# Seven products for the last block's projection, and an earlier spread of the first block's attention

## Chip, cores and metric

One core of a Trainium2 chip. The metric is the device time of the kernel in microseconds (us); lower is better.

## The reference

```python
# q, k, v: (8 batches, 8 heads, 576 tokens, 64)
scores = q @ k.T / 8 + bias(head, distance), masked to 0 <= distance < 128
x      = softmax(scores) @ v             # heads joined: 4608 tokens x 512
g, val = x @ w_gate, x @ w_val           # 512 -> 1536
out    = (silu(g) * val) @ w_out         # 1536 -> 512, float32
```

## The kernel before

The 4608 tokens are nine blocks of 512 (block 8 is made of the last 64 tokens of all eight batches). For a block, attention makes four tiles `x`, TensorE transposes them (`px`, copied to `xT`), and twelve columns of the FFN follow: a gate group `pg`, a value group `pv` (four matmuls of 512 each), ScalarE's `tt`, VectorE's `uu` and `hT`. Then the block is projected by `w_out` (`po`). In attention, `pt` is the transpose of a tile of k or q (loaded as `kn`, `qn`), `ps` and `psc` are the scores, and `av` is their product with v; the rank of a tile is its place in the order of use. All of it is one list of steps in which attention steps of later blocks are mixed with FFN steps of the present one. A scheduler turns the list into one fixed instruction order for each engine, using its own idea of durations; on the chip each engine then takes its instructions in that order.

How far attention is pushed ahead is the target. `b1` is 24, `ALONE` is 8, so this is one attention step an FFN step from 8, and three from 16:

```python
if step < b1:
    target = base + max(0, step - ALONE) + max(0, step - 16) * (32 - b1 + ALONE) / (b1 - 16)
...
while (n_att < target or done < ready[blk]) and att_step():
    pass
```

The loads are issued by GpSimd. k and q of ranks 9 and 10 are issued later from within the steps, so they stand in the queue behind `w_out` (two loads of 768 KB, issued at 40.36 and 41.83 us; k and q follow from 42.64):

```python
load(7)
load(8)
loaded = 9
for a0 in (0, 6):
    nc.gpsimd.dma_start(wo_sb[:, a0:a0 + 6, :], wo2[:, a0:a0 + 6, :])
```

Block 0 is projected plainly during block 1.

```python
def project(n, j, pool, tag, bufs):
    po = pool.tile([P, DM], FP32, name="po", tag=tag, bufs=bufs)
    for m0 in range(0, NMB, 4):
        for i in range(m0, m0 + 4):
            m = NMB - 1 - i if n == 0 else i
            nc.tensor.matmul(po, hT[n][:, m, j * P:(j + 1) * P], wo_sb[:, m, :],
                             start=(i == 0), stop=(i == NMB - 1))
        ...
```

Blocks 1 to 7 are projected with seven products instead of eight (`strassen`, a Winograd form: halves of tokens, of columns of `hT`, and of columns of `w_out`; `sums` makes the sums of `hT` on VectorE; the code below is condensed, with lines joined and helpers left out). Block 8 was the exception: three tiles by `project`, the last by `last_project` in two halves of 256 columns.

```python
def strassen(n, t):                      # t: one of two halves, called in turn
    po = ps_f.tile([P, 2, HC], FP32, name="po", tag="po", bufs=1)
    ...
    X, Y = po[:, 0, :], po[:, 1, :]      # two accumulators, one tile
    product(X, A11, B11, True);  nc.scalar.mul(p1s, X, 0.5);         yield
    product(p2, A12, B21, True); half_plus(top[:, 0:HC], p2, p1s);   yield
    product(X, S2, T2);          nc.scalar.mul(u2s, X, 0.5);         yield
    product(Y, S1, T1);          nc.scalar.mul(p5s, Y, 0.5);         yield
    product(X, S3, T3);          half_plus(low[:, HC:DM], X, p5s);   yield
    product(Y, S4, B22);         half_plus(top[:, HC:DM], Y, u2s);   yield
    product(X, A22, T4);         nc.scalar.mul(low[:, 0:HC], X, 0.5)
    # stores of top and low
```

The softmax here doesn't subtract the row's maximum and nothing guards it: scores larger than these inputs give would overflow.

Of the kernel before, what the change touches and what calls it, by code (L numbers as in the profile page):

```python
# [10 lines left out]
FP32 = mybir.dt.float32  # L11
# [5 lines left out]
P = 128  # L17
# [4 lines left out]
ALONE = 8  # L22
# [25 lines left out]
def kernel(  # L48
# [10 lines left out]
    nc = tc.nc  # L59
    B, H, S, D = q.shape  # L60
    NTOK, DM = out.shape
    DFF = moe_w_gate.shape[1]
    NKB = DM // P
    NMB = DFF // P
    NSUP = B // 2
    NBLK = NTOK // 512
# [50 lines left out]
    wo_sb = consts.tile([P, NMB, DM], FP16, name="wo_sb")  # L117
# [9 lines left out]
    supool = ctx.enter_context(tc.tile_pool(name="sup", bufs=4))  # L127
    opool = ctx.enter_context(tc.tile_pool(name="op", bufs=8))
    ps_f = ctx.enter_context(tc.tile_pool(name="ps_f", bufs=3, space=PSUM))
    ps_a = ctx.enter_context(tc.tile_pool(name="ps_a", bufs=4, space=PSUM))  # L130
# [225 lines left out]
    hT = {}  # L356
# [36 lines left out]
    def gate_val(n, m):  # L393
        c0 = 384 if (n, m) in acted else 0
        gate(n, m, wide(n, m, "g"), c0)
        yield
        val(n, m, wide(n, m, "v"), c0)
        yield

    def rows_of(n, j):  # L400
        if n == 8:
            return [(0, 64, 2 * j * S + 512), (64, 128, (2 * j + 1) * S + 512)]
        return [(0, 128, n * S + j * P)]

    def project(n, j, pool, tag, bufs):
        po = pool.tile([P, DM], FP32, name="po", tag=tag, bufs=bufs)
        for m0 in range(0, NMB, 4):
# [4 lines that stand above are left out]
            if m0 + 4 == NMB:  # L412
                osb = opool.tile([P, DM], FP32, name="osb", tag="osb")
                nc.scalar.mul(osb, po, 0.5)
                for p0, p1, r0 in rows_of(n, j):
                    nc.sync.dma_start(out[r0:r0 + p1 - p0, :], osb[p0:p1, :])
            yield

    def last_project(n, j):

        osb = opool.tile([P, DM], FP32, name="osb", tag="osb")
        for half in range(2):
            c = slice(half * DM // 2, (half + 1) * DM // 2)
            po = ps_a.tile([P, DM // 2], FP32, name="po", tag="a", bufs=4)
            for m in range(NMB):
                nc.tensor.matmul(po, hT[n][:, m, j * P:(j + 1) * P], wo_sb[:, m, c],
                                 start=(m == 0), stop=(m == NMB - 1))
            if half == 0:
                nc.scalar.mul(osb[:, c], po, 0.5)
            else:  # L430
                nc.vector.tensor_scalar_mul(osb[:, c], po, 0.5)
            for i, (p0, p1, r0) in enumerate(rows_of(n, j)):
                (nc.sync if i == 0 else nc.scalar).dma_start(out[r0:r0 + p1 - p0, c], osb[p0:p1, c])
            yield 1.5



# [2 lines left out]
    HC = DM // 2  # L440
# [4 lines left out]
    def weight_sums(c):  # L445

        if c == 0:
            one_more.append(supool.tile([P, 1], FP32, name="one", tag="pin", bufs=1))
            nc.vector.memset(one_more[0], 1.0)
        k = slice(2 * c, 2 * c + 2)  # L450
        for t_, a, b in ((T1, B12, B11), (T3, B22, B12)):
            nc.vector.scalar_tensor_tensor(out=t_[:, k, :], in0=a[:, k, :], scalar=one_more[0],
                                           in1=b[:, k, :], op0=ALU.mult, op1=ALU.subtract)
        nc.vector.tensor_sub(T2[:, k, :], B22[:, k, :], T1[:, k, :])
        nc.vector.tensor_sub(T4[:, k, :], B21[:, k, :], T2[:, k, :])
# [17 lines left out]
    def strassen(n, t):  # L473

        h = hT[n]
        A11, A12 = h[:, 0:HM, 0:256], h[:, HM:NMB, 0:256]
        S1, A22 = h[:, 0:HM, 256:512], h[:, HM:NMB, 256:512]
        S2, S3, S4 = hsum[n]
        cols = slice(t * P, (t + 1) * P)
        po = ps_f.tile([P, 2, HC], FP32, name="po", tag="po", bufs=1)  # L480
        p2 = ps_a.tile([P, HC], FP32, name="p2", tag="a")
        top, low = (opool.tile([P, DM], FP32, name="osb", tag="osb") for _ in range(2))
        p1s = supool.tile([P, HC], FP32, name="p1s", tag="p1s", bufs=1)
        p5s = supool.tile([P, HC], FP32, name="p5s", tag="p5s", bufs=1)
        u2s = supool.tile([P, HC], FP32, name="u2s", tag="u2s", bufs=1)

        def product(dst, a, b, start=False):
            for m in range(HM):
                nc.tensor.matmul(dst, a[:, m, cols], b[:, m, :], start=(start and m == 0),  # L489
                                 stop=(m == HM - 1), skip_group_check=True)  # L490

        def half_plus(dst, a, b):
            nc.vector.scalar_tensor_tensor(out=dst, in0=a, scalar=0.5, in1=b,
                                           op0=ALU.mult, op1=ALU.add)

        X, Y = po[:, 0, :], po[:, 1, :]
        product(X, A11, B11, True)
        nc.scalar.mul(p1s, X, 0.5)
        yield
        product(p2, A12, B21, True)  # L500
        half_plus(top[:, 0:HC], p2, p1s)
        yield
        product(X, S2, T2)
        nc.scalar.mul(u2s, X, 0.5)
        yield
        product(Y, S1, T1)
        nc.scalar.mul(p5s, Y, 0.5)  # L507
        yield
        product(X, S3, T3)
        half_plus(low[:, HC:DM], X, p5s)  # L510
        yield
        product(Y, S4, B22)
        half_plus(top[:, HC:DM], Y, u2s)
        yield
        product(X, A22, T4)
        nc.scalar.mul(low[:, 0:HC], X, 0.5)
        for j, osb in ((t, top), (t + 2, low)):
            for p0, p1, r0 in rows_of(n, j):
                nc.sync.dma_start(out[r0:r0 + p1 - p0, :], osb[p0:p1, :])
        yield  # L520



    AT = {2, 3, *range(5, 10), *range(11, 18)}
# [1 line left out]
    def ffn():  # L526

        for n in range(NBLK):
            if n > 1:
                parts = chain(strassen(n - 1, 0), strassen(n - 1, 1))  # L530
            if n == 1:
                for j in range(PRE):
                    for _ in project(0, j, ps_f, "po", 1):
                        yield 1.0
            for m in range(NMB):
                for half, _ in enumerate(gate_val(n, m)):
                    yield 1.0
                    if n > 1 and 2 * m + half in AT:
                        next(parts)
                        yield 0.75  # L540
                if n == 1:
                    if m % 2 and PRE + m // 2 < 4:
                        for _ in project(0, PRE + m // 2, ps_f, "po", 1):
                            yield 1.0
                    if m in (2, 4, 6):
                        weight_sums(m // 2 - 1)
                if 0 < n < NBLK - 1 and m >= 9:
                    sums(n, m - 9)
            if n > 1:
                assert next(parts, None) is None  # L550
        for j in range(3):
            for _ in project(NBLK - 1, j, ps_a, "a", 4):
                yield 1.0
        yield from last_project(NBLK - 1, 3)


    loaded = done_t = 0
# [126 lines left out]
    def everything():  # L684
        nonlocal done
        base = 0
        busy(WARM)
        with tc.manual_schedule(engines=ENGINES[MANUAL]):
            first_tiles()
            done = FIRST  # L690
            steps = progress(ffn())
            while (at := next(steps)) < ALONE:
                if at == 2.0:
                    nc.scalar.copy(idm2, idm)
        for step in steps:
            if step == MASKS_AT:
                make_masks()

            b1 = 24 + 3 * PRE

            lead = LEAD if done < X_DMA_FROM - 2 else LEAD + 4
            blk = (0 if step + LEAD < b1 else 1 if step + LEAD < 60
                   else min(NBLK - 1, 2 + int((step + lead - 60) // 34.5)))
            if step < b1:

                target = base + max(0, step - ALONE) + max(0, step - 16) * (32 - b1 + ALONE) / (b1 - 16)
            elif step < 60:
                target = base + 32 + SECOND * 8 * (step - b1) / (60 - b1)
            else:
                target = base + 32 + SECOND * 8 + (step - 60) * RATE * 8 / 34.5  # L710
            while (n_att < target or done < ready[blk]) and att_step():
                pass
# [32 lines left out]
```

## Time and profile before

| | before |
|---|---|
| time, median of 3 runs | 356.27 us (356.26 to 356.39) |
| span in the profile | 354.5 us |
| TensorE busy | 341.5 us, 96% |
| clock granted to TensorE | 1.00 throughout |
| last matmul ends, tail after it | 350.54, 3.92 us |
| first `pg` of block 1 | 56.93 us |

TensorE is the bound, so the tables and lines below are read for two things only: how long TensorE's next instruction waits, and how long the span goes on after its last one. The lines for this are in the prediction.

### The profile page before, as it was taken

The page shows a single profiled execution, that of the slowest core. Times are in us where ns is not written, and L with a number is a line of the kernel's source. Part 1 is how long each engine was busy: PE and PEld are TensorE (multiplying, and loading weights), DVE is VectorE, ACT ScalarE, POOL GpSimd, SP SyncE. Part 2 cuts the span into 40 slices and gives each one's busy share as a digit, 9 for nine tenths or more (in the row PEclk, how much of TensorE's full clock was granted, in tenths as well). Part 3 has the DMA queues.
Part 4 walks back from the last instruction along what each step waited for, and adds up shares of the span by engine and source line. Part 5 has one row for each costly group of instructions (what it writes and reads, how often), then busy time and mean ns, then how long its engine had stood idle before and what let it go on. Part 6 is the DMA issues. An engine that isn't in the chain of part 4 may idle for free.

```text
span 354.5 us, 7261 instructions
## 1 busy us (share of the span) xinstructions
PE 341.5 (96%) x2765; PEld 197.5 (56%) x2765; DVE 273.4 (77%) x599; ACT 178.9 (50%) x355; POOL 106.9 (30%) x132
## 2 busy tenths in 40 slices
PE   7889999999999999999999999999999999999995
PEld 4684555444456655565456555664665566556643
DVE  4867976997987799678986998799878965975540
ACT  6845584555555455665556455455444323332321
POOL 8966655544848445544300100000000000000000
PEclk9999999999999999999999999999999999999999
DMA  9999999999999999999995513311022101101114
GB/s 152 170 186 187 141 176 155 99 147 137 157 142 196 146 158 163 157 167 153 165 62 105 83 39 32 88 33 58 17 75 61 44 2 59 62 0 62 41 42 96
DMA packets 157763, 37.34 MB, mean 105 GB/s; under 512 B 147232, under 2 KB 153248, under 8 KB 157728
## 3 DMA queue, kind: packets, MB, share of 16 engines
q0 software_dynamic: 116224, 18.62, 79.8%
q1 hardware_dynamic: 41056, 17.97, 27.6%
q8 instruction: 21, 0.34, 0.4%
q10 hardware_dynamic: 448, 0.30, 0.3%
q14 instruction: 14, 0.11, 0.1%
HBM read 37.91 MB, written 9.44 MB: 134 GB/s over the span
## 4 chain that ended last, share of the span: by engine, by line
PE 73%; DVE 16%; ACT 7%; issue 3%; DVEq 0%; ACTq 0%
PE pv L369 20%; PE pg L369 20%; PE po L489 14%; PE av L320 4%; DVE uu L384 4%; DVE hT L391 3%; PE ps L255 3%; PE po L410 3%; DVE ex L264 3%; PE p L489 2%; ACT ex L260 2%; PE px L346 2%; ACT tt L383 2%; ACT exc L287 2%; DVE x L323 1%
## 5 line engine op out<-in xcount | busy, mean ns | idle before, releaser
L369 PE MATMUL pg<-xT,wg_sb 128*128 128x512 f16 (+2 forms) x464 | 116.0, 365 | 0.6 <-DVE uu L384 0.3
L369 PE MATMUL pv<-xT,wv_sb 128*128 128x512 f16 (+2 forms) x464 | 114.5, 364 | 0.8 <-DVE uu L384 0.4
L383 ACT ACTIVATE tt<-pg 128x512 f16<-128x512 f32 (+2 forms) x110 | 65.5, 596 | 85.2 <-PE pg L369 81.8
L384 DVE SCALAR_TENSOR_TENSOR uu<-tt,pg 128x512 f16<-128x512 f16 (+2 forms) x109 | 73.4, 674 | 34.6 <-ACT tt L383 33.9
L391 DVE TENSOR_TENSOR hT<-uu,pv 128x512 f16<-128x512 f16 (+2 forms) x110 | 74.0, 673 | 7.1 <-PE pv L369 2.2
L369 PEld LDWEIGHTS <-wv_sb 128*128 128x128 f16 x464 | 42.8, 98 | 37.4 <-issue 3.3
L369 PEld LDWEIGHTS <-wg_sb 128*128 128x128 f16 x464 | 42.5, 98 | 36.1 <-issue 3.5
L260 ACT ACTIVATE ex<-ps 128x512 f16<-128x512 f32 x96 | 50.2, 605 | 10.1 <-PE ps L255 10.1
L169 POOL DMA_DIRECT2D va<-in_v_dram x40 | 34.1, 856 | 53.0 <-PE av L320 36.9
L175 POOL DMA_DIRECT2D qn<-in_q_dram x39 | 33.6, 864 | 24.4 <-DMA qT<-qn 14.8
L175 POOL DMA_DIRECT2D kn<-in_k_dram x39 | 33.2, 859 | 25.7 <-DMA kT<-kn 18.4
L264 DVE TENSOR_TENSOR ex<-ex,m_reg 128x1024 f16<-128x1024 f16 x48 | 32.6, 687 | 10.3 <-ACT ex L260 10.3
L489 PEld LDWEIGHTS <-hT 128*128 128x128 f16 x336 | 31.8, 98 | 15.5 <-issue 3.6
L489 PEld LDWEIGHTS <-S 128*128 128x128 f16 x252 | 23.9, 98 | 11.8 <-issue 2.9
L323 DVE TENSOR_TENSOR x<-av,rec 128x256 f16<-128x256 f32 x72 | 29.0, 420 | 0.6
L489 PE MATMUL po<-T,hT 128*128 128x256 f16 x168 | 23.1, 272 | 0.5
L489 PE MATMUL po<-T,S 128*128 128x256 f16 x168 | 23.0, 273 | 0.6 <-ACT p5s L507 0.6
L287 ACT ACTIVATE exc<-psc 128x512 f16<-128x512 f32 x40 | 21.4, 608 | 3.4 <-PE psc L283 3.4
L347 ACT COPY xT<-px 128x512 f16<-128x512 f16 x24 | 14.1, 586 | 14.9 <-PE px L346 14.8
L320 PEld LDWEIGHTS <-ex 128*128 128x128 f16 x384 | 18.4, 97 | 4.9 <-issue 0.7
L320 PE MATMUL av<-va,ex 128*128 128x65 f16 x384 | 20.4, 193 | 0.5
L410 PE MATMUL po<-wo_sb,hT 128*128 128x512 f16 x84 | 19.7, 379 | 0.0
(74 smaller groups left out, 291.0 us busy)
## 6 DMA issues: line engine op xcount, KB each, us to landing
out_dram<-osb SPq DMA_DIRECT2D x32, 256.0 KB, 2.8
va<-in_v_dram POOLq DMA_DIRECT2D x32, 128.0 KB, 7.5
qn<-in_q_dram POOLq DMA_DIRECT2D x31, 128.0 KB, 8.2
kn<-in_k_dram POOLq DMA_DIRECT2D x31, 128.0 KB, 8.1
wo_sb<-in_moe_w_out_dram POOLq DMA_DIRECT2D x2, 768.0 KB, 9.3
wg_sb<-in_moe_w_gate_dram POOLq DMA_DIRECT2D x2, 512.0 KB, 10.5
wv_sb<-in_moe_w_val_dram POOLq DMA_DIRECT2D x2, 512.0 KB, 11.8
out_dram<-osb SPq DMA_DIRECT2D x6, 128.0 KB, 2.4
```

What stands on the lines that cost most here:

```text
L169: nc.gpsimd.dma_start(va[rank][p0:p1, :, 0:D], src)
L175: nc.gpsimd.dma_start(t_[p0:p1], src)
L260: nc.scalar.activation(e[:, o:o + 2, :], banks[q4][par], AF.Exp, scale=scale)
L264: nc.vector.tensor_mul(e[:, o, :], e[:, o, :], reg[:, o, :])
L320: nc.tensor.matmul(av[:, j, :], w, val, start=(n == 0), stop=(n == len(todo) - 1))
L323: nc.vector.tensor_mul(x[:, 4 * half:4 * half + 4, :], av[:, :, 0:D], rec.broadcast_to([P, 4, D]))
L369: nc.tensor.matmul(ps[:, c0:c1], w[:, kb, ms], xT[n][:, kb, c0:c1], start=(kb == 0 and c0 == 0), stop=(kb == NKB - 1 and c1 == 512), skip_ ...
L383: nc.scalar.activation(tt, pg[:, c0:c1], AF.Tanh, scale=0.5)
L384: nc.vector.scalar_tensor_tensor(out=uu, in0=tt, scalar=one if (n, m) == PIN else 1.0, in1=pg[:, c0:c1], op0=ALU.add, op1=ALU.mult)
L391: nc.vector.tensor_mul(hT[n][:, m, c0:c1], acted[(n, m)][1][:, c0:c1], pv[:, c0:c1])
L410: nc.tensor.matmul(po, hT[n][:, m, j * P:(j + 1) * P], wo_sb[:, m, :], start=(i == 0), stop=(i == NMB - 1))
L489: nc.tensor.matmul(dst, a[:, m, cols], b[:, m, :], start=(start and m == 0), stop=(m == HM - 1), skip_group_check=True)
```

## The change

Part 1, attention of the first block: the same 32 steps by step 24, but 1.5 for each FFN step from 8 and 2.5 from 16, to make the burst before block 1 smaller. Part 2, the last block: seven products as in the other blocks, 84 matmuls of 256 columns instead of 36 of 512 and 24 of 256; the two halves `t` alternate, the last scaling is VectorE's, and the stores go out on two queues. The diff is cut.

```diff
-                if 0 < n < NBLK - 1 and m >= 9:
+                if n > 0 and m >= 9:
                     sums(n, m - 9)
...
-        for j in range(3):
-            for _ in project(NBLK - 1, j, ps_a, "a", 4):
-                yield 1.0
-        yield from last_project(NBLK - 1, 3)
+        ends = [strassen(NBLK - 1, t) for t in range(2)]
+        for t in 7 * (0, 1):
+            next(ends[t])
+            yield 0.75
...  (in strassen)
+        pool, tag, bufs = (ps_a, "a", 4) if end and t else (ps_f, "po", 1)
+        if end and t:
+            store(n, t + 2, low, HC, DM, True)       # after the fifth product
+        store(n, t, top, 0, DM, end)                 # after the sixth
-        nc.scalar.mul(low[:, 0:HC], X, 0.5)
+        if end:
+            nc.vector.tensor_scalar_mul(low[:, 0:HC], X, 0.5)
+        else:
+            nc.scalar.mul(low[:, 0:HC], X, 0.5)
+        store(n, t + 2, low, 0, HC if end and t else DM, end)
...
-                target = base + max(0, step - ALONE) + max(0, step - 16) * (32 - b1 + ALONE) / (b1 - 16)
+                target = base + 1.5 * max(0, step - ALONE) + max(0, step - 16)
```

More of the change, by code (lines that the diff above doesn't have):

```diff
@@ L403, in rows_of, with store @@
         return [(0, 128, n * S + j * P)]
+    def store(n, j, osb, c0=0, c1=512, two=False):
+        for i, (p0, p1, r0) in enumerate(rows_of(n, j)):
+            (nc.scalar if two and i else nc.sync).dma_start(out[r0:r0 + p1 - p0, c0:c1],
+                                                            osb[p0:p1, c0:c1])
     def project(n, j, pool, tag, bufs):
@@ L414, in project @@
                 nc.scalar.mul(osb, po, 0.5)
-                for p0, p1, r0 in rows_of(n, j):
-                    nc.sync.dma_start(out[r0:r0 + p1 - p0, :], osb[p0:p1, :])
+                store(n, j, osb)
             yield
-    def last_project(n, j):
-        osb = opool.tile([P, DM], FP32, name="osb", tag="osb")
-        for half in range(2):
-            c = slice(half * DM // 2, (half + 1) * DM // 2)
-            po = ps_a.tile([P, DM // 2], FP32, name="po", tag="a", bufs=4)
-            for m in range(NMB):
-                nc.tensor.matmul(po, hT[n][:, m, j * P:(j + 1) * P], wo_sb[:, m, c],
-                                 start=(m == 0), stop=(m == NMB - 1))
-            if half == 0:
-                nc.scalar.mul(osb[:, c], po, 0.5)
-            else:
-                nc.vector.tensor_scalar_mul(osb[:, c], po, 0.5)
-            for i, (p0, p1, r0) in enumerate(rows_of(n, j)):
-                (nc.sync if i == 0 else nc.scalar).dma_start(out[r0:r0 + p1 - p0, c], osb[p0:p1, c])
-            yield 1.5
     HM = NMB // 2
@@ L479, in strassen @@
         cols = slice(t * P, (t + 1) * P)
-        po = ps_f.tile([P, 2, HC], FP32, name="po", tag="po", bufs=1)
+        end = n == NBLK - 1
+        pool, tag, bufs = (ps_a, "a", 4) if end and t else (ps_f, "po", 1)
+        po = pool.tile([P, 2, HC], FP32, name="po", tag=tag, bufs=bufs)
         p2 = ps_a.tile([P, HC], FP32, name="p2", tag="a")
         top, low = (opool.tile([P, DM], FP32, name="osb", tag="osb") for _ in range(2))
-        p1s = supool.tile([P, HC], FP32, name="p1s", tag="p1s", bufs=1)
-        p5s = supool.tile([P, HC], FP32, name="p5s", tag="p5s", bufs=1)
-        u2s = supool.tile([P, HC], FP32, name="u2s", tag="u2s", bufs=1)
+        if end and t:
+            spare = [opool.tile([P, DM], FP32, name="osb", tag="osb") for _ in range(2)]
+            p1s, p5s, u2s = spare[0][:, 0:HC], spare[0][:, HC:DM], spare[1][:, 0:HC]
+        else:
+            p1s, p5s, u2s = (supool.tile([P, HC], FP32, name=i, tag=i, bufs=1)
+                             for i in ("p1s", "p5s", "u2s"))
         def product(dst, a, b, start=False):
@@ L510, in strassen @@
         half_plus(low[:, HC:DM], X, p5s)
+        if end and t:
+            store(n, t + 2, low, HC, DM, True)
         yield
@@ L513, in strassen @@
         half_plus(top[:, HC:DM], Y, u2s)
+        store(n, t, top, 0, DM, end)
         yield
         product(X, A22, T4)
-        nc.scalar.mul(low[:, 0:HC], X, 0.5)
-        for j, osb in ((t, top), (t + 2, low)):
-            for p0, p1, r0 in rows_of(n, j):
-                nc.sync.dma_start(out[r0:r0 + p1 - p0, :], osb[p0:p1, :])
+        if end:
+            nc.vector.tensor_scalar_mul(low[:, 0:HC], X, 0.5)
+        else:
+            nc.scalar.mul(low[:, 0:HC], X, 0.5)
+        store(n, t + 2, low, 0, HC if end and t else DM, end)
         yield
```

## The prediction

> **What bounds the kernel now.** I began with the busy times by engine and the chain that ended last, then read the end in order of time, then the stretch from 24 to 90 us, since the change touches only the first block's attention and the last block's projection.
>
> ```profile
> PE 341.5 (96%) x2765; PEld 197.5 (56%) x2765; DVE 273.4 (77%) x599; ACT 178.9 (50%) x355; POOL 106.9 (30%) x132
> PE 73%; DVE 16%; ACT 7%; issue 3%; DVEq 0%; ACTq 0%
> ...
> 340.15 7.77 PE po L410 x36
> 347.92 2.63 PE po L426 x24
> ```
>
> TensorE is busy 96% of the span and makes 73% of the chain; its granted clock is 1.00 in all stretches I read. The two last lines are the chain's last links: the last block's plain projection, 10.40 us of TensorE with no wait in it. This is how the kernel ends, in order of time:
>
> ```profile
> 339.99 7.93 PE L410 MATMUL po<-wo_sb,hT 128*128 128x512 f16 x36
> ...
> 340.81 0.69 DVE L391 TENSOR_TENSOR hT<-uu,pv 128x512 f16<-128x512 f16 x1
> ...
> 347.76 2.78 PE L426 MATMUL po<-wo_sb,hT 128*128 128x256 f16 x24
> ...
> 350.58 0.42 DVE L431 TENSOR_SCALAR osb<-po 128x256 f32<-128x256 f32 x1 [9.08 <-PE po L426]
> ```
>
> The last product ends at 350.54, VectorE scales it by 351.01, two stores of 64 rows go out at 351.03, their packets run from 352.15 to 352.88, and the span ends at 354.46. So the tail after TensorE is 3.92 us, and its packets end 2.34 us after TensorE. The other end of the matter, the first block:
>
> ```profile
> 52.25 0.28 PE L346 MATMUL px<-idm,x 128*128 128x128 f16 x2 [0.32 <-DVE x L323]
> ...
> 53.82 1.89 PE L410 MATMUL po<-wo_sb,hT 128*128 128x512 f16 x8
> ...
> 55.64 0.29 PE L346 MATMUL px<-idm,x 128*128 128x128 f16 x2
> ...
> 56.93 1.02 PE L369 MATMUL pg<-xT,wg_sb 128*128 128x512 f16 x4
> 58.62 0.75 DVE L384 SCALAR_TENSOR_TENSOR uu<-tt,one,pg 128x512 f16<-128x512 f16 x1 [2.71 <-ACT tt L383]
> ```
>
> Attention ends in a burst: TensorE waits for VectorE's x at 51.3 (0.40), 52.25 (0.32) and 53.6 (0.24); then eight projection products fill the time until the last x is there. VectorE is idle for 2.71 us at the seam to block 1 and then without a gap until 77.9.
>
> [...] the starts of the last products are 216 and 109 ns apart; [...] the last two stores, on two queues, moved 128 KB in 0.73 us. [...]the stores here land 2.0 to 2.5 us after issue with the data included.
>
> **The last block, TensorE.** Removed: 36 products of 512 columns, 36 x 216 = 7.78 us, and 24 of 256, 24 x 109 = 2.62; sum 10.40. Added: two column halves, seven products each, of six matmuls of 256 columns: 84 x 109 = 9.16 us. Gain 1.24 us. Wait at the seam: the second product needs the last hT, and VectorE now also makes the twelve sums. I counted them on with the step that the same sums have one block earlier:
>
> ```profile
> 301.64 0.75 DVE L468 TENSOR_TENSOR S<-hT 128x512 f16<-128x512 f16 x2
> 302.31 0.42 DVE L469 TENSOR_TENSOR hT<-hT 128x512 f16<-128x512 f16 x1
> 302.64 0.42 DVE L468 TENSOR_TENSOR S<-hT 128x512 f16<-128x512 f16 x1
> 303.07 0.69 DVE L384 SCALAR_TENSOR_TENSOR uu<-tt,pg 128x512 f16<-128x512 f16 x1
> ```
>
> A sum takes 0.34 us in a row, 0.46 where it needs the one before. In the order of the changed program six of them stand between the gates of columns 8 and 10, and three more before the last hT. That puts the gate of 10 at 338.45 (before: 338.29), its end at 339.13, which the last pv needs for its PSUM buffer (0.07 us of wait), and the last hT at 341.8 instead of 341.5. Meanwhile TensorE does the two first products, which need only the first six columns, and five sixths of the third, to 341.9. So the wait there is 0.1 us or less. S4 is ready some 3 us before its product. Each accumulator is read 0.4 us after its product while the other half runs 0.65 us, so the alternation hides every eviction. TensorE thus ends 1.24 - 0.14 = 1.1 us earlier.
>
> **The last block, tail.** The scaling of the last 256 columns is on VectorE in both kernels, 0.42 us, and its last store has the same size, so with free queues the tail would stay at 3.92. But the stores bunch. Before, 256 KB every 2.6 us; after, all 1 MB within the last 2.6 us: half of low(1), top(0), top(1), low(0), half of low(1), issued at -2.1, -1.5, -0.8, -0.2 and +0.5 us from TensorE's end (0.65 us a product, 0.49 for VectorE and issue). The rate for stores of block 8 and of an ordinary block:
>
> ```profile
> 323.00:325.60 2.60, 2.60 (x19) 1.65 (x17) 0.89 (x2) 0.98 (x2) 0.00 (x0) 1.00 0.54 202
> 344.60:346.10 1.50, 1.50 (x9) 0.68 (x8) 0.00 (x0) 0.60 (x1) 0.00 (x0) 1.00 0.82 175
> ```
>
> The two last columns are DMA share and GB/s. A 128-row store runs 256 KB in 0.83 us (packets of 2 KB at 87 ns); block 8 writes 64 rows to each of two batches, packets of 152 ns, 1.43 us with the ramp, so some 1.28 in a row (8 packets an engine x 160). Data begin 1.1 us after issue: low(1) from -1.0 to -0.3, then 256 KB each to +1.0, +2.3, +3.5, and the last half to +4.2, against +2.34 before: 1.8 us more tail. If the two queues overlapped perfectly (87 ns) the last packets would end at about +2.6, 0.3 more. Mixed packets in the last stores average 70 ns per KB between the 46 and 85 of the extremes, so I take 1.5. Last block together: -1.1 + 1.5 = +0.4 us.
>
> **The first block.** The target is now 1.5 steps per FFN step from 8 and 2.5 from 16, where it was 1 and 3. Both give 32 at step 24, but at step 18 tile 8 must be done anyway (37 steps), so the burst begins with 17 steps behind it instead of 14. The order of instructions shows what this is: exactly one pg/pv pair (1.73 us of TensorE, 1.3 of VectorE) moves from before the burst into its end, and from about 90 us to the last block nothing is reordered. Four pg matmuls now stand in the three gaps above (0.40, 0.32, 0.24): 0.75 us won. The hold at 34.75 (0.37, pv behind VectorE) lies where the pair was and may go: 0.2. Against that, only four pv (0.86 us) instead of eight po (1.73) stand between the last av and the last px: px then waits about 0.9, and the next pg, behind two copies on ScalarE, about 0.5 more; so 1.2 us lost over the 0.2 that stands there. In return VectorE does the pair and two copies, 2.1 us, in its hole of 2.71, so block 1 starts with less behind it: of the waits of TensorE from 57 to 90, 2.0 us in my count of start-to-start gaps, I give back a third, 0.7. Sum: -0.75 - 0.2 + 1.2 - 0.7 = -0.45 us. Loads are no limit for the earlier transposes: k of rank 5 lands at 29.6, its transpose moves from 35.6 to about 33.5.
>
> **Sum.** 356.27 + 0.4 - 0.45 = 356.2. A version that was kept is more likely to have been the better one, and both of my losses (stores in a row, px) are estimates that could be smaller, so I shift by 0.4 to 355.8.
>
> **Rivals.** (a) *The stores drain freely.* [...] +0.3 instead of +1.5. For it: in the last 128 KB a third of the packets take 46 ns. Against: the others take 80 to 90. Then 354.6. (b) *VectorE becomes the bound in the last block*: the sums delay the last hT by a full microsecond and TensorE waits. For it: 9 sums are fitted between three gates. Against: gates wait 0.25 to 1.65 us for ScalarE there today, so there is room. Then +0.8, 356.6. (c) *The pair is better where it was*: the filler lost at 54 us costs all of its 1.4 us and VectorE's hole gives nothing back. Then 356.9. (d) *The burst gets clear*: all gaps from 33 to 57 us shrink (3.2 us in my count), and block 1 starts 1.2 us sooner for good. Then 354.7.
>
> **Range and chances.** Last block: -0.8 to +1.2; first block: -1.6 to +0.9. They are independent, so I take 354.4 to 357.2. Two per cent is 7.1 us; all that the change touches, even with every wait gone, is under 6. Faster 0.02, same 0.97, slower 0.01.
>
> **What would show it.** Right: 84 products of 109 ns, TensorE's end 1.1 us nearer to the start of the first of them, a wait of at most 0.1 in front of the third; tail near 5.4 us with the DMA busy without a hole until 1.9 us before the end. First block: three small gaps gone at 50 to 53 us, a new wait at px before block 1, VectorE's hole of 2.7 us mostly filled. Wrong: a tail of 4.2 us or less (rival a), a wait over 0.5 us before the third product (b), or block 1 starting more than 1.5 us earlier or later than 56.9.

The sum came to 356.2, shifted to 355.8.

## The result

The changed kernel took 361.86 us, the median of four runs (360.63 to 362.1), against 356.3 for the kernel before on the same chip (356.26 to 356.39): a ratio of 1.0149, 95% interval 1.0125 to 1.0172. It was predicted at 355.8, so it is 6.1 us off and outside the range of 354.4 to 357.2, though within 2% of the kernel before. (Ratios here are the mean time of one kernel's fast runs over that of the other's in the same rounds, so not quite the ratio of the medians quoted.)

The page of the changed kernel, the lines on busy time, the granted clock in 40 slices, and the shares of the chain that ended last:

```profile
PE 342.1 (95%) x2789; PEld 199.7 (56%) x2789; DVE 280.7 (78%) x618; ACT 178.7 (50%) x357; POOL 106.7 (30%) x132
...
PEclk9999996999999999999999999999999999999999
...
PE 75%; DVE 10%; ACT 6%; DMA 4%; issue 2%; POOL 0%; SPq 0%; DVEq 0%; ACTq 0%
```

Two things are new: a slice with the clock at six tenths, the seventh (54 to 63 us), and DMA in the chain, with 4%. Both point to one place. I lined up the starts of the 464 `pg` matmuls of the two traces: the changed kernel is 0.1 us behind until 33 us, 0.8 at the 61st, 6.2 at the 89th, 5.4 at the 97th, and then 5.3 to 5.4 to the last. Lags in between come in part from matmuls that were moved. Counted in matmul work already started, the two kernels are within 0.2 us of each other from 49 to 51 us and 5.4 us apart at 64. So the loss arises between 48 and 67 us, the seam from block 0 to block 1, and little is lost or won in the blocks after.

Busy times by stretch there, before and then after; the columns are stretch, length, busy us of PE, PEld, DVE, ACT and POOL, the granted clock, DMA share (the time of all packets over that of 16 engines, so over 1 where packets overlap) and GB/s:

```profile
48.00:55.00 7.00, 6.25 (x86) 3.67 (x84) 6.01 (x15) 6.01 (x12) 2.63 (x3) 1.00 1.72 169
55.00:57.00 2.00, 2.00 (x14) 0.86 (x12) 0.91 (x3) 0.65 (x2) 1.61 (x2) 1.00 2.48 154
57.00:63.00 6.00, 6.00 (x36) 2.99 (x36) 4.24 (x8) 2.80 (x5) 1.89 (x3) 1.00 2.50 155
```

```profile
48.00:55.00 7.00, 5.48 (x68) 2.88 (x68) 6.17 (x15) 4.87 (x10) 2.44 (x3) 1.00 1.64 167
55.00:57.00 2.00, 1.11 (x10) 0.68 (x9) 0.55 (x2) 1.17 (x2) 1.80 (x3) 0.64 2.47 154
57.00:63.00 6.00, 4.70 (x16) 2.05 (x17) 2.29 (x5) 0.60 (x1) 3.45 (x4) 0.55 2.49 154
```

From 57 to 63 us TensorE made 36 matmuls before and 16 after, and "busy" hides most of it: at half clock a matmul of 512 columns takes twice the time (427 ns from start to start against 216) and counts as busy all along. The timeline of the changed kernel says what TensorE waited for. In brackets stand the idle time just before the line and what ended it:

```profile
54.01 0.28 PE L346 MATMUL px<-idm,x 128*128 128x128 f16 x2 [0.79 <-DVE x L323]
...
54.90 0.40 PE L202 MATMUL pt<-idm,kn 128*128 128x128 f16 x4 [0.60 <-DMA kn<-in_k_dram]
...
55.59 0.29 PE L202 MATMUL pt<-idm,qn 128*128 128x128 f16 x1 [0.29 <-DMA qn<-in_q_dram]
...
58.30 0.61 PE L202 MATMUL pt<-idm,qn 128*128 128x128 f16 x4 [1.89 <-DMA qn<-in_q_dram]
...
58.70 1.91 PE L369 MATMUL pg<-xT,wg_sb 128*128 128x512 f16 x4
60.40 1.91 PE L369 MATMUL pv<-xT,wv_sb 128*128 128x512 f16 x4
62.11 1.18 PE L369 MATMUL pg<-xT,wg_sb 128*128 128x512 f16 x4
```

The first wait was predicted. The other three are transposes of k and q of ranks 9 and 10 that stand in front of block 1's first `pg` and wait for their loads, which landed at 54.85, 55.54 and 58.25. Before, all but one of the same transposes came later, behind block 1's first matmuls, and waited for nothing (in the same view of the kernel before):

```profile
56.74 0.22 PE L202 MATMUL pt<-idm,kn 128*128 128x128 f16 x1
...
61.24 0.33 PE L202 MATMUL pt<-idm,kn 128*128 128x128 f16 x3
61.41 0.61 PE L202 MATMUL pt<-idm,qn 128*128 128x128 f16 x8
```

There the loads landed at 53.57, 54.52 and 57.46, 0.8 to 1.3 us sooner; but above all the users moved forward: q of rank 10 was used after 61.4 before, and is wanted by about 56.2 now.

A second cost comes with it. The granted clock, in stretches cut at its changes:

```profile
52.16:55.57 3.41, 1.74 (x17) 0.67 (x13) 2.50 (x7) 1.46 (x4) 1.31 (x2) 1.00 2.39 157
55.57:62.40 6.83, 4.92 (x19) 2.32 (x20) 2.24 (x5) 1.53 (x3) 4.82 (x6) 0.50 2.47 155
62.40:67.00 4.60, 4.60 (x22) 2.06 (x21) 4.45 (x9) 0.82 (x2) 0.00 (x0) 1.00 2.62 128
```

For 6.83 us the clock was half: a 512-column matmul starts every 427 ns in it instead of every 216. In the records of the clock, the stretches at full clock are 51.20 and 296.96 us long in this kernel and 348.16 in the kernel before; with the 6.83 these are 15, 87, 102 and 2 times 3.413 us. In the 3.41 us before the fall TensorE was not idle: it was busy 1.74 of them. In the four runs a lower mean clock goes with a longer time: three have 0.990 to 0.991 and take 361.66 to 362.1, the fourth, with 0.995, takes 360.63. In `part1_only` below it does so less clearly: one run with 0.994 takes 361.6, another 361.09.

The sum closes to some tenths. Start to start, TensorE's waits beyond the pitch are 0.95 for `px`, and 0.76, 0.46 and 2.14 for the loads, together 3.36. Eight matmuls at half clock lose 0.21 each and one transpose part of that, 1.8. That makes 6.1; less 0.6 to 0.9 won nearby (the gaps in the burst), it is the 5.3 seen.

The last block went as planned on TensorE. From the last `pg` to TensorE's end it took 10.57 us, 1.06 less than the 11.63 before. After TensorE's end the span lasts 5.05 us, against 3.92.

### The profile page after: what moved, and what is told of

Same layout as the page of the kernel before. It is cut to its first block, busy times and chain, and to the rows that moved or that the text cites. A ratio compares the mean times of both kernels' runs of the same rounds, so it can differ in the third digit from the quotient of the medians.

```text
span 359.8 us, 7334 instructions
## 1 busy us (share of the span) xinstructions
PE 342.1 (95%) x2789; PEld 199.7 (56%) x2789; DVE 280.7 (78%) x618; ACT 178.7 (50%) x357; POOL 106.7 (30%) x132
## 4 chain that ended last, share of the span: by engine, by line
PE 75%; DVE 10%; ACT 6%; DMA 4%; issue 2%; POOL 0%; SPq 0%; DVEq 0%; ACTq 0%
PE pv L369 22%; PE pg L369 22%; PE po L481 16%; PE av L320 4%; PE ps L255 3%; DMA qn<-in_q_dram 3%; PE p L481 3%; ACT ex L260 3%; DVE hT L391 2%; PE po L415 2%; DVE uu L384 2%; PE px L346 2%; DVE ex L264 2%; ACT tt L383 1%; DMA stage<-in_q_dram 1%
## 5 line engine op out<-in xcount | busy, mean ns | idle before, releaser
L369 PE MATMUL pg<-xT,wg_sb 128*128 128x512 f16 (+2 forms) x464 | 117.3, 367 | 0.6 <-DVE uu L384 0.3
L481 PEld LDWEIGHTS <-hT 128*128 128x128 f16 x384 | 36.4, 98 | 16.3 <-issue 3.5
L481 PEld LDWEIGHTS <-S 128*128 128x128 f16 x288 | 27.4, 98 | 12.3 <-issue 2.9
L481 PE MATMUL po<-T,S 128*128 128x256 f16 x192 | 26.0, 273 | 0.6 <-ACT p5s L499 0.6
L481 PE MATMUL po<-T,hT 128*128 128x256 f16 x192 | 26.1, 272 | 0.5
L255 PE MATMUL ps<-qT,kT 64*128 64x256 f16 x192 | 17.3, 272 | 1.5 <-DVE qT L207 0.8
```

What stands on the lines that cost most here:

```text
L255: nc.tensor.matmul(two[par][:, j, :], kT[rows, ks, pair, :], qT[rows, p:p + 2, pair, :], start=(j == 0), stop=(j == 1))
L369: nc.tensor.matmul(ps[:, c0:c1], w[:, kb, ms], xT[n][:, kb, c0:c1], start=(kb == 0 and c0 == 0), stop=(kb == NKB - 1 and c1 == 512), skip_ ...
L481: nc.tensor.matmul(dst, a[:, m, cols], b[:, m, :], start=(start and m == 0), stop=(m == HM - 1), skip_group_check=True)
```

## The experiments

The theory at the start, L in the expectations: the transposes moved in front of loads that had not landed, and the half clock that followed, cost all of it. Rivals: the burst itself, with one FFN pair more in it, by VectorE and ScalarE (F); or the last block's end (E). The runs of one group shared a chip and the runs of the kernel before.

### Each part alone

`part1_only` is the kernel before with the new line for the target, `part2_only` the change without it.

```diff
# part1_only, against before
-                target = base + max(0, step - ALONE) + max(0, step - 16) * (32 - b1 + ALONE) / (b1 - 16)
+                target = base + 1.5 * max(0, step - ALONE) + max(0, step - 16)
```

> The kernel before with only the spread of the first block's attention changed; the last block keeps its plain projection. Theory L (late loads: the new order puts the transposes of k and q of ranks 9 and 10 ahead of block 1's products, and TensorE waits for their loads, then runs at half clock): the whole loss is here, 361.6 us, within 0.8, with the same waits at 53 to 58 us and a clock of 0.5 until about 62. Rival E (the end of the kernel, its bunched stores, makes the loss): 356.3 and no low clock.

> The kernel before with only the last block's seven products. Theory L: neutral, 356.3 within 0.4, because the end of TensorE comes 1.1 us earlier and the tail is 1.1 us longer (5.05 against 3.92), as the trace of the changed kernel shows. Rival E: about 361. My prediction's own sum for this part was 356.7.

`part1_only`: 361.61 us, ratio 1.0151 (1.0135 to 1.0166). `part2_only`: 355.94 us, ratio 0.9995 (0.998 to 1.0009). The first part alone has the whole loss: waits at the same places (0.95 for `px`, 1.43, 0.54 and 2.15 for the three loads) and again 6.83 us of half clock. The second part alone is not told apart from the kernel before. Its TensorE ends at 349.21 and its span at 354.20. What the seven products win is given back behind them:

```profile
347.04 3.34 SPq L407 DMA_DIRECT2D out_dram<-osb  x5
347.05 3.62 ACTq L407 DMA_DIRECT2D out_dram<-osb  x5
...
347.74 1.47 PE L481 MATMUL po<-T,hT 128*128 128x256 f16 x12
...
349.25 0.42 DVE L512 TENSOR_SCALAR osb<-po 128x256 f32<-128x256 f32 x1 [0.23 <-PE po L481]
```

All ten store issues fall within 3.6 us. From the transfers of that end, summed by queue: 1 MB in 4.2 us, that is 245 KB/us, with packets of 2 KB at 109 ns (in the changed kernel's trace 4.22 us, 243 KB/us and 109 ns). With the tail at 4.99 instead of 3.92 us this is 1.1 us more, and cancels the 1.06 of TensorE. (The expectation of `one_store` has 4.94, counted to the start of the last instruction.)

### The loads ahead of w_out

Is it the loads? In `loads_first` k and q of ranks 9 and 10 are issued before `w_out`; TensorE's order is instruction by instruction that of the changed kernel. In `q10_first` this is done for q of rank 10 alone, whose wait was the longest.

```diff
# loads_first, against the changed kernel     # q10_first: only load_qk(10, "q") ahead
     load(8)
+    load_qk(9)
+    load_qk(10)
     loaded = 9
     for a0 in (0, 6):
         nc.gpsimd.dma_start(wo_sb[:, a0:a0 + 6, :], wo2[:, a0:a0 + 6, :])
...
-        load_qk(rank)
+        if rank not in (9, 10):
+            load_qk(rank)
```

> The changed kernel with k and q of ranks 9 and 10 loaded ahead of the two loads of w_out; the order of TensorE's instructions is word for word that of the changed kernel. Theory L: the waits of 0.76, 0.46 and 2.14 us and the half clock go, the wait of 0.95 us for x stays; 355.8 to 356.6. Rival F (the loss comes from the pair that moved and its missing filler, in whatever order the loads come): over 358.

> The changed kernel with q of rank 10 alone ahead of w_out; same order on TensorE. It tells the last wait (2.14 us) from the two before it. k and q of rank 9 come one load (0.9 us) later, to 55.8 and 56.5. Theory L: the wait for q10 goes, those for rank 9 grow by some 0.9, so 1.2 to 1.7 us less than the changed kernel, 360.0 to 360.6, if the clock falls as before; 358.5 if it does not. If the clock drop has another cause than idle time, nothing changes in it.

`loads_first`: 356.57 us, ratio 1.0013 (0.9998 to 1.0028): the 5 us are gone, with the burst, VectorE's and ScalarE's work and the order of TensorE unchanged. The clock stays at 1.00. What TensorE still waits for between 48 and 67 us, in the view of waits (total, times, longest), is the rest of theory and prediction, `px` and the first `pg` behind its copies on ScalarE:

```profile
PE px L347 <- DVE x L324: 0.8, 1, 0.8
PE pg L370 <- ACT xT L348: 0.6, 1, 0.6
```

Start to start these two are 0.95 and 0.77. So part 1 gains nothing in this trace even where no load is in its way: at the last `pg` it is 0.4 us behind the kernel before, where I had it 0.45 ahead.

`q10_first`: 360.62 us, ratio 1.0136 (1.0118 to 1.0154). Taking away the longest of three waits brought back about 1 of 5 us in the trace; by the ratios it is 0.5 us, and the intervals of the two kernels overlap. The wait for q of rank 10 is gone, but the queue is one row: k of rank 9, now behind one load more, made TensorE wait 2.41 us in place of 0.76, and q of rank 9 0.61. The clock fell for 3.41 us from 56.34, instead of 6.83. The loads stand in one queue, so here the waits had to be removed together.

### Why the order changed

The steps of these transposes stand where they stood in the program's list. What puts them ahead of block 1's matmuls? My second theory: the scheduler fills the hole at the seam. Before, `po` matmuls of block 0 filled it. With one `pg`/`pv` pair moved into the end of the burst, block 0's last `hT` column comes later, and since `project(0)` begins its sum with just that column, no `po` can be used; the scheduler takes the transposes, for which it must have reckoned the loads as landed (this last I infer; no run shows its reckoning). `forward` tests it with one line: the sum begins with the first column. `t1250` asks whether the loss grows with the amount moved or is a switch.

```diff
# forward, against the changed kernel
-                m = NMB - 1 - i if n == 0 else i
+                m = i
# t1250, against the changed kernel
-                target = base + 1.5 * max(0, step - ALONE) + max(0, step - 16)
+                target = base + 1.25 * max(0, step - ALONE) + 1.5 * max(0, step - 16)
```

> The changed kernel with one line altered: the projection of block 0 sums its columns from the first instead of from the last. In the program order built from it the projection's matmuls are again available as filler while the last hT column of block 0 is outstanding, and the k and q transposes of ranks 9 and 10 stand behind block 1's first pg, as in the kernel before. Theory (the moved pair makes the last column late, the projection that starts with that column cannot fill, and transposes whose loads have not landed are put in its place): no TensorE wait over 0.3 us on a load between 48 and 67 us, no stretch of half clock, 355.5 to 356.5 us. Rival (the burst itself, with one pair more in it, costs the 5 us, through VectorE or ScalarE): 360 us or more.

> The changed kernel with the target's slopes at 1.25 and 1.5 steps instead of 1.5 and 1 (1 and 1 plus 2 in effect before): a smaller shift of attention. The order built from it has the transposes of ranks 9 and 10 late, as before. Theory (the cost is a switch in the order, not the amount of attention moved): 355.5 to 356.6 us, no half clock. Rival (the cost grows with the amount moved): about half of the loss, 358 to 359 us.

`forward`: 355.62 us, ratio 0.9977 (0.9965 to 0.999), faster than the kernel before, and by 6 us than the changed kernel. Its seam:

```profile
53.68 0.28 PE L346 MATMUL px<-idm,x 128*128 128x128 f16 x2
...
53.80 0.38 PE L415 MATMUL po<-wo_sb,hT 128*128 128x512 f16 x1
...
54.13 1.03 PE L415 MATMUL po<-wo_sb,hT 128*128 128x512 f16 x4
...
54.99 1.03 PE L369 MATMUL pg<-xT,wg_sb 128*128 128x512 f16 x4
...
59.96 0.39 PE L202 MATMUL pt<-idm,kn 128*128 128x128 f16 x4
...
60.18 0.61 PE L202 MATMUL pt<-idm,qn 128*128 128x128 f16 x8
```

Nine `po` matmuls stand around the last `px` (the first four at 52.72, just before these lines), the transposes are back at 60 us, and the view of TensorE's waits names none from 48 to 67 us: not for loads, and not for `px` or the first `pg` either. The gaps of 0.40 and 0.24 that the kernel before had at 51.3 and 53.6 are gone as well. At the last `pg` TensorE is 0.97 us ahead of the kernel before (with the difference of the first `pg` taken off), where `part2_only`, counted in the same way, is 0.09 ahead. So the earlier spread and the forward sum together are worth some 0.9 us in the trace. The obvious rival, the forward sum with the old spread, was not run. Its order, which was only built, has `po` matmuls in the same three gaps, and it too has these transposes ahead of block 1's first `pg`; why, was not looked into. So how the 0.9 divides stays open.

`t1250`: 356.29 us, ratio 0.9997 (0.9985 to 1.001). Its transposes are late, no clock falls, and the gaps of 0.39 and 0.24 stand as before. Built but not run, a slope of 1.125 gave TensorE the order of `t1250`; 1.75 and 2.0 put the transposes ahead of block 1's first `pg`, as 1.5 does. At the two slopes that were run the loss is nothing or all, as a switch in the order would have it.

### The end: spacing the stores

Of the last block's two halves, one done first would let its stores leave early. `halves_apart` does five products of half 0 and then five of half 1, after two of each; `one_store` puts each store of two 64-row pieces into one transfer from 128 partitions; `apart_one` has both.

```diff
# halves_apart, against part2_only
-        for t in 7 * (0, 1):
+        for t in (0, 1, 0, 1) + 5 * (0,) + 5 * (1,):
# one_store, against part2_only, in store()
+        if n == NBLK - 1:
+            nc.sync.dma_start(out.rearrange("(b s) d -> b s d", s=S)[2 * j:2 * j + 2, 512:576, c0:c1],
+                              osb[:, c0:c1])
+            return
```

> As part2_only, but after two products of each column half the first half is finished before the second goes on, so that its stores leave 3 us earlier. Theory B (bunching): only 512 KB are issued in the last 1.3 us, tail 4.4 to 4.6, time 355.4 to 355.6, if TensorE keeps its pace. Rival W (the alternation was needed to hide the evictions): TensorE waits between products of one half and its end comes over 0.5 us later, time 356.0 or more.

> The last block's seven products in the old attention order (as part2_only), but each store of a half block is one transfer from all 128 partitions to the two stretches of the output, in place of two of 64 partitions on two queues. Theory P (the tail is bound by the packets of the 64-partition stores, 109 ns each where a 128-partition store has 87): the megabyte drains in about 3.4 us in place of 4.2, the tail falls from 4.94 to 4.1 to 4.3, time 355.1 to 355.4. Rival B (bunching alone: what counts is that all stores are issued in the last 2.6 us, in whatever form): 355.9.

> Both of the above. If packets and bunching each cost what their theories say and there is no wait, the last store meets an empty queue: tail 4.0, time 354.9 to 355.1, the gain of 1.1 us of TensorE nearly whole. If only one of them matters, no better than the better of the two.

`halves_apart`: 357.85 us, ratio 1.0046 (1.0032 to 1.006). The tail fell to 3.9 us, which speaks for the bunching as what makes it long. But TensorE waited 2.8 us in the last block, counted from start to start beyond the pitch. The view of its waits, which counts only what lies between modelled ends, names them:

```profile
PE po L481 <- DVE osb L485: 1.4, 3, 0.6
PE po L481 <- ACT p5s L499: 0.3, 1, 0.3
```

The alternation of the halves had hidden every eviction; without it, each product waits for the read of the one before, because both accumulators of a half are one tile.

`one_store`: 373.86 us, ratio 1.0497 (1.0483 to 1.0512), and `apart_one` 374.31 us, ratio 1.051. A plain miss. The view of the transfers from 353 to 371 us, long after TensorE's end:

```profile
DMA  0111111111111111111111111111111111111111
...
q1 hardware_dynamic: 512, 0.90, 13.0%
```

The third number is the share of the 16 engines: 13%, 2.1 engines' worth. In `part2_only` the stores of 64 rows kept the engines busy at 7 to 9 tenths for most of their time. The stores here differ from those in form (one transfer from 128 partitions to 2 batches x 64 rows) and in queue (SyncE's alone); what leaves two engines at work was not shown. I had looked at the 128 partitions of the source only. Of the five issues the first three took 0.5 to 0.7 us, the last two 5.56 and 4.79.

### The last scaling on ScalarE

```diff
# scalar_scale, against part2_only
-        if end:
-            nc.vector.tensor_scalar_mul(low[:, 0:HC], X, 0.5)
-        else:
-            nc.scalar.mul(low[:, 0:HC], X, 0.5)
+        nc.scalar.mul(low[:, 0:HC], X, 0.5)
```

> As part2_only, but the last sums are scaled by ScalarE (0.38 us) in place of VectorE (0.42). If the choice of engine matters because ScalarE also issues five of the ten last stores (0.55 to 0.78 us each, in order), the last scaling waits behind an issue and the time grows by 0.3 to 0.8 us, 356.2 to 356.7. If only the duration matters: 355.9, the same.

356.23 us, ratio 1.0004 (0.9992 to 1.0017). Beside the 0.9995 of `part2_only`, this is 0.3 us in favour of VectorE and not resolved: the intervals overlap. The wait that was asked about is there in the trace: ScalarE's last scaling begins 0.45 us after TensorE's end, behind a store issue (349.22 to 349.90) and the scaling before it, where VectorE's begins 0.04 after it.

### A better end

`apart_two_banks` gives `Y` a tile of its own, and keeps the halves apart. `combined` is `forward` with that end and with the stores of half 0 on SyncE's queue alone.

```diff
# apart_two_banks, against part2_only
+        py = ps_f.tile([P, HC], FP32, name="py", tag="gv") if end else None
-        X, Y = po[:, 0, :], po[:, 1, :]
+        X, Y = po[:, 0, :], py if end else po[:, 1, :]
-        product(Y, S1, T1)
+        product(Y, S1, T1, end)
-        for t in 7 * (0, 1):
+        for t in (0, 1, 0, 1) + 5 * (0,) + 5 * (1,):
# combined, against forward: the same, and
-        store(n, t, top, 0, DM, end)
+        store(n, t, top, 0, DM, end and t)
-        store(n, t + 2, low, 0, HC if end and t else DM, end)
+        store(n, t + 2, low, 0, HC if end and t else DM, end and t)
```

> The last-block part alone, with the products of the two column halves ordered so that half 0 finishes two products before half 1 has its last ones (order 0 1 0 1, then five of half 0, then five of half 1), and with the two accumulators of a half in two PSUM tiles of their own. Theory: the earlier try of this order lost its gain because the two accumulators shared one tile, so every product waited for the read of the other one; with tiles apart TensorE ends as in the last-block part alone (349.2 us), and the stores, spaced over twice the time, leave a tail of 3.9 to 4.5 us: 354.9 to 355.5 us. Rival (a half on its own waits for its evictions whatever the tiles, as X and Y are each read 0.4 us after a product and needed again one product later): TensorE ends 0.7 to 1.5 us later, 355.8 to 356.8 us.

> A candidate to beat both kernels: the changed kernel with block 0's projection summed from the first column (as in the run before, 0.9977 of the kernel before), and at the end the halves apart (order 0 1 0 1, five of half 0, five of half 1), the accumulators in two PSUM tiles, and the stores of half 0 all issued by SyncE. In the run with the halves apart in two tiles TensorE waited 1.40 us because ScalarE was held in two store issues (0.58 and 1.49 us) in front of the two evictions of half 1. Theory: with the issues off ScalarE that wait goes, TensorE's time from block 9's first product to its end is as in the alternating order, and the tail falls from 5 to some 4 to 4.5 us: ratio to the kernel before 0.995 to 0.9965, 354.5 to 355.1 us. Rival: half 0's stores, 64 rows at a time from one queue, take until those of half 1 begin (1.3 us each, so 3.2 us for the two and a half left), and the tail stays near 5 us: ratio 0.9975.

`apart_two_banks`: 356.97 us, ratio 1.0014 (1.0001 to 1.0028). The waits for evictions of half 0 went with the shared tile, as expected, but one of 1.40 us, start to start, appeared where neither theory had it:

```profile
345.87 2.18 ACTq L407 DMA_DIRECT2D out_dram<-osb  x2
...
348.18 0.38 ACT L497 ACTIVATE osb<-po 128x256 f32<-128x256 f32 x1 [3.67 <-DMA out_dram<-osb]
...
348.61 0.81 PE L482 MATMUL po<-T,S 128*128 128x256 f16 x6 [1.23 <-ACT osb L497]
```

ScalarE issued two stores of half 0 (0.58 and 1.49 us) in front of the two evictions of half 1, and TensorE needed those.

`combined`: 355.14 us, ratio 0.9966 (0.9953 to 0.998). With the issues on SyncE no wait over 0.1 us is left in TensorE's last block. Yet the span in the profile is 353.3, against 353.5 of `forward`, with TensorE's end the same within 0.02 us: half 0's stores of 64 rows, now on one queue, take until half 1's begin, so the tail stays near 5 us (4.93; 5.10 in `forward`), as the rival said. It is the fastest run here, 1.0 us below the kernel before, but its interval overlaps that of `forward`, and I would not claim the end's part of it.

## Why the prediction was wrong

- **Which step failed.** "The order of instructions shows what this is: exactly one pg/pv pair [...] moves from before the burst into its end" and "Loads are no limit for the earlier transposes". I had compared the order for `pg` and `pv` and checked one load, k of rank 5. The transposes of ranks 9 and 10 also moved, ahead of block 1's first `pg`, and their loads were the limit: 3.36 us of waits and 1.8 us of half clock. `loads_first` shows this by taking the loads out of the way, `forward` by taking the transposes out of it. The order of the changed kernel was there to read before it ran.
- **Why they moved.** My text saw that "only four pv (0.86 us) instead of eight po (1.73) stand between the last av and the last px" and priced it as a wait for `px`. It did not ask what the scheduler would put there. The wait of 0.9 was right (0.95); what came in the rest of the hole was not considered. That with this spread the backward sum of `project(0)` keeps the `po` out is shown by `forward`; why that sum runs backward I do not know.
- **The other terms of the first block.** "the next pg, behind two copies on ScalarE, about 0.5 more" is 0.77 in `loads_first`. "Four pg matmuls now stand in the three gaps" held: the gaps at 51.3 and 53.6 are gone in the changed kernel and in `forward`. (The one at 53.6 stands in front of an `av`, not of a `px`; the view names no wait for x there.) The 0.37 at 34.75 did not go; one of 0.56 stands at 35.5 instead. The 0.7 given back for block 1 did not come, as rival (c) had it: from its first `pg` to the 32nd after it TensorE's start-to-start waits are 1.8 us before and 1.8 in `loads_first`. All terms together were to be -0.45; without loads in the way they are about +0.4 in the trace, and -0.9 with the hole filled.
- **Range.** The first block was to be -1.6 to +0.9. None of my rivals for the first block had a load or the clock in it: (c), the nearest, priced the lost filler at 1.4 us. The statement "block 1 starting more than 1.5 us earlier or later than 56.9" was named as what would make the prediction wrong, and block 1's first `pg` indeed starts at 58.70.
- **The last block, right.** TensorE 1.06 us sooner (predicted 1.1), no wait before the third product and none for evictions, so rival (b) falls. The tail grew by 1.1 us (predicted 1.5, with 0.3 for rival (a)): two queues moved 245 KB/us, where the 64-row stores of the kernel before, on one queue, moved 179 (256 KB in 1.43 us). The sum had them in a row. Sum +0.0 instead of +0.4; `part2_only` measures 0.9995.
- **The shift by 0.4** for "a version that was kept" pushed the wrong way. The version is 1.5% slower.

## What to carry to other kernels

Where a scheduler fixes each engine's order, a small move in one place can let it pull other work forward (here transposes that then waited 3.36 us for their loads); compare the whole order at the place of the move, and check every load that the pulled instructions need, above all those behind large ones in the same queue (issued ahead of these, in `loads_first`, they cost no wait). Keep work that needs nothing new, such as a sum over early columns, available at such a seam. A saving at the very end counts only as far as the last stores do not bunch (in `part2_only` 1.1 us more tail took back 1.06 us of TensorE), and a store's issue can itself hold the engine that someone is waiting for (1.40 us of TensorE in `apart_two_banks`).

## What else the runs measured

- Stores of 64 rows on two queues moved 245 KB/us over the last megabyte (`part2_only`), and such stores in a row on one queue 179 (256 KB, kernel before) and 187 (384 KB, `combined`): 31 to 37% more. The last pair of the kernel before, 128 KB in 0.73 us on two queues, that is 175 KB/us, shows nothing of it.
- The clock. I cut each run, from the changes of its clock, into stretches of 3.413 us. The clock fell after a stretch in which TensorE was busy 1.74 us (changed kernel, with no single wait over 0.95 us before the fall), 1.35 (`part1_only`) and 0.39 (`q10_first`). It stayed full after the two stretches at the seam in `loads_first`, 2.61 and 2.81, and after every other stretch at full clock until TensorE's end; the least busy of these had 2.03 in the changed kernel (from 4.37 us) and 1.96 in `combined` (from 4.03 us). So in these runs the fall came at 1.74 us and less and not at 1.96 and more, if the modelled busy times are right. What decides it was not shown.
- At full clock 512-column matmuls in a row start every 216 ns (kernel before, the last 36: 7.77 us).
- The issues of stores to a destination of 2 x 64 rows grew: to 5.56 us after three of 0.5 to 0.7 (`one_store`). Issues of 64-row stores on ScalarE's queue varied from 0.5 to 1.5 us when stores were bunched, which delayed ScalarE's own work (TensorE waited 1.40 us in `apart_two_banks`).
